# Four of the eight transfers of the first w_in piece issued from ScalarE's queue instead of SyncE's

## The chip, the core and the metric

The kernel runs on one NeuronCore of a Trainium2 chip. The metric is the device time of one execution in microseconds (us), the median of several runs. The core has five engines with an instruction stream each: TensorE (PE; its weight loads are shown as PEld), VectorE (DVE), ScalarE (ACT), GpSimd (POOL) and SyncE (SP). In this kernel transfers from and to memory are issued from SP's stream and, for a few, from ACT's.

## The reference

A gated linear recurrence over 4 batches of 8 heads, 768 steps, 48 features, and a feed-forward block on its output (3072 tokens of 384 features, 2048 hidden).

```python
state = np.zeros((B, H, D, D), dtype=np.float32)
for t in range(S):
    state = alpha[:, :, t, :, None] * state + np.einsum('bhd,bhe->bhde', k[:, :, t], v[:, :, t])
    y[:, :, t] = np.einsum('bhd,bhde->bhe', q[:, :, t], state)
...
x = np.ascontiguousarray(y.transpose(0, 2, 1, 3)).reshape(B * S, H * D)
h = x @ w_in
g = h - np.tanh(h)
return (g @ w_out).astype(np.float32)
```

The weights w_in and w_out come as 64-bit floating point numbers; all else is 32-bit.

## The kernel before, in words

The tokens are worked in 12 units of 256 (`TU`), three to a batch. Each unit has two parts. The recurrence (`gla`) turns alpha, k and q so that features lie on partitions, scans alpha from both ends on DVE (`scan_U` L711, `scan_W` L730), scales k by U and q by W (`times` L679), and then for each chunk of 128 tokens forms scores on PE (`scores`), masks them on DVE (`masked`), multiplies by v (`products`) and updates the state. The feed-forward part (`moe`) runs 8 steps per unit: `first` (six matmuls with w_in, L1081, out tile h), four operations on ACT and DVE that form g, and `second` (matmuls with w_out, L1126 for units 0 and 1, L1147 with fewer products from unit 2 on). Unit 0's and 1's steps are numbered 0 to 15 here in the order in which they run.

The weights arrive in 16 pieces during unit 0 and 1's work. A piece of w_in is eight transfers (six of 48 partitions, two of 16), one of w_out is one; `load_weight` (L39 to L44) issues them, all on SP. A piece holds raw 64-bit numbers; `round_weight` makes 32-bit ones of them with two operations on ACT (L86, L87) and two on DVE (L89, L90), here called the conversion of the piece. It writes the tile `w_in[:, :, 2*s*128 : 2*(s+1)*128]`, that is a stretch in each of three rows j, which interleave with those of other pieces.

At the very start the eight loads of unit 0's alpha, k, q and v are issued in halves, one half each from SP and ACT (L595, L584). Then SP goes on with the first piece of w_in (L43), unit 1's alpha (L600), the second piece, and so on. The program gives eight semaphores to these transfers in turn, so that each transfer waits until the one that had its semaphore before has landed. ACT's stream holds, after its four loads, a table load and a small wake-up operation (L478), then the copy of alpha's first half out of PSUM into tile aT (`place`, L670); DVE copies the second half into the same tile, alternate columns of it.

The order of all this is not written by hand. Every piece of work is a task with an engine, an estimated time, a rank and the tasks that it needs. `Planner.order` simulates the engines with these estimates, eight times with changed priorities, keeps the best plan and emits the tasks in the order of their planned starts; each engine runs its own in that order. `plan.begin` (L1211) says at what time each engine is free for planned work. Where the plan leaves PE idle ahead of the first products (task "y 0.0"), `spin` (L1209) fills in matmuls of the identity with itself, one for each 0.24 us of planned idle time.

The task `fetch` (L566) of a piece carries the time that its issues are thought to take on SP: 5.7 for the first two pieces, 4.3 for later ones of w_in, 2.0 for w_out.

Of the kernel before, what the change touches and what calls it, by code (L numbers as in the profile page):

```python
# [35 lines left out]
R_MAX = 2.0 ** 60  # L36


def load_weight(nc, pool, rows, **kw):  # L39

    raw = pool.tile([P, WN], I64 if rows[0][2].dtype != FP32 else FP32, name="raw", **kw)
    for at, js, src in rows:
        nc.sync.dma_start(out=raw[at].rearrange("p (j n) -> p j n", n=src.shape[-1])[:, js], in_=src)  # L43
    return raw  # L44


def weight_parts(w_in, w_out, pad_rows, what, s, by_tile=True):

    if what == "out":
        return [(slice(0, P), slice(0, 2), w_out.rearrange("(j p) n -> p j n", p=P)[:, 2 * s:2 * s + 2, :])]  # L50
    parts = []
    for i in range(len(pad_rows[0])):
        at, f0 = pad_rows[0][i]
        step = pad_rows[1][i][1] - f0
        src = w_in[f0:f0 + len(pad_rows) * step].rearrange("(j p) n -> p j n", p=step)
        src = src[0:at.stop - at.start, :, 2 * s * P:2 * (s + 1) * P]

        few = at.stop - at.start < 32 or not by_tile
        parts += [(0, at, slice(0, len(pad_rows)), src)] if few else [(j - 9, at, slice(j, j + 1), src[:, j:j + 1]) for j in range(len(pad_rows))]
    return [x[1:] for x in sorted(parts, key=lambda x: (x[0], x[1].start))]  # L60
# [73 lines left out]
def general(tc, q, k, v, alpha, moe_w_in, moe_w_out, out, w_in, w_out, ident, pad_rows):  # L134
# [10 lines left out]
    with ExitStack() as ctx:  # L145
        with tc.tile_pool(name="g_raw", bufs=1) as raw_pool:
            for s in range(FT // 2):
                for what, dst in (("in", w_in[:, :, 2 * s * P:2 * (s + 1) * P]), ("out", w_out[:, 2 * s:2 * s + 2, :])):
                    raw = load_weight(nc, raw_pool, weight_parts(moe_w_in, moe_w_out, pad_rows, what, s))
                    round_any_weight(nc, raw_pool, raw, dst)  # L150
# [171 lines left out]
class Planner:  # L322
# [13 lines left out]
    def add(self, name, engine, us, rank, after, do, lat=0.3):  # L336
        kind = name.rsplit(" ", 1)[0]
        self.tasks.append((name, engine, us, rank, [a for a in after if a], do, lat, self.last.get(kind)))
        self.last[kind] = name
# [85 lines left out]
def fast(tc, q, k, v, alpha, moe_w_in, moe_w_out, out, w_in, w_out, ident, ok, pad_rows):  # L425
    nc = tc.nc
# [12 lines left out]
    V, A, T, GP = nc.vector, nc.scalar, nc.tensor, nc.gpsimd  # L439
# [3 lines left out]
    with ExitStack() as ctx:  # L443
# [7 lines left out]
        raw_pool = incoming.enter_context(tc.tile_pool(name="incoming", bufs=2))  # L451
# [83 lines left out]
        plan = Planner()  # L535
        add = plan.add
# [11 lines left out]
        pieces = sorted(((what, s) for s in range(FS) for what in RANK), key=lambda x: (RANK[x[0]] + 2 * x[1], x))  # L548
        raw_of = {}

        def fetch(what, s):
            raw_of[what, s] = load_weight(nc, raw_pool, weight_parts(moe_w_in, moe_w_out, pad_rows, what, s), bufs=4)

        def convert(what, s):
            it = []

            def begin():
                dst = w_in[:, :, 2 * s * P:2 * (s + 1) * P] if what == "in" else w_out[:, 2 * s:2 * s + 2, :]
                it.append(round_weight(nc, raw_pool, raw_of.pop((what, s)), dst))
                next(it[0])  # L560
            return begin, lambda: next(it[0], None)

        for n, (what, s) in enumerate(pieces):
            rank = RANK[what] + 2 * s
            held = pieces[n - 4] if n >= 4 else None
            add(f"fetch {what}{s}", "SP", 5.7 if n < 2 else 4.3 if what == "in" else 2.0, rank - 30, [held and f"read {held[0]}{held[1]}"],  # L566
                lambda what=what, s=s: fetch(what, s), lat=2.5)
            a, b = convert(what, s)
            older = pieces[n - 2] if n >= 2 else None
            add(f"read {what}{s}", "ACT", 1.9, rank, [f"fetch {what}{s}", older and f"{older[0]}{older[1]}"], a)  # L570
            add(f"{what}{s}", "DVE", 1.6, rank, [f"read {what}{s}"], b)
# [480 lines left out]
        def reload(n):  # L1052
            looked[n] = load_weight(nc, combo_pool[0], weight_parts(moe_w_in, moe_w_out, pad_rows, *pieces[n], by_tile=False))
# [4 lines left out]
        for n in range(len(pieces)):  # L1058
            rank = 2 * FS * 3 + 8 * n
# [148 lines left out]
                spun.append(ps_o.tile([P, P], FP32, name="spin", tag="o2"))  # L1208
            T.matmul(spun[0], lhsT=ident, rhs=ident, start=True, stop=True)  # L1209
        plan.filler = "PE", "y 0.0", 0.24, spin  # L1210
        plan.begin.update(SP=0.8, PE=1.5, ACT=3.0, DVE=4.8)  # L1211

        for u in range(NU):
            gla(u, rank_gla(u))
# [44 lines left out]
def kernel(  # L1259
# [28 lines left out]
    w_out = consts.tile([P, FT, d_model], FP32, name="w_out")  # L1288
    ok = consts.tile([1, 1], I32, name="ok")
    fine = fast(tc, q, k, v, alpha, moe_w_in, moe_w_out, out, w_in, w_out, ident, ok, pad_rows)  # L1290
    with tc.If(fine < 1):
        general(tc, q, k, v, alpha, moe_w_in, moe_w_out, out, w_in, w_out, ident, pad_rows)
# [30 lines left out]
```

## Time and profile before

| what | us |
|---|---|
| median of 3 runs (lowest, highest) | 578.11 (577.57, 578.14) |
| the profiled execution's own time | 578.14 |
| its span in the profile | 576.4 |
| PE busy, share of the span | 568.0, 99% |
| DVE busy | 451.0, 78% |
| ACT busy | 322.8, 56% |
| first matmul of `first` (L1081) starts at | 31.23 |
| fillers (L1209) before that, matmuls | 46 |

In the profile a 32-bit matmul shows as two records, so that 18 fillers are "x36". Times in its rows are us from the start of the span. A row of the timeline gives the start, the length, the engine, the line, the operation with its tiles and shapes, how many are merged, and in brackets how long the engine sat idle before and what ended that. "SPq" and "ACTq" are issues of transfers from the streams of SP and ACT.

### The profile page before, as it was taken

To read this page: it belongs to the slowest core of one execution; us is meant where nothing else is said; L and a number is where in the kernel's file an instruction comes from. 1 tells how busy PE (TensorE), PEld (TensorE's weight loads), DVE (VectorE), ACT (ScalarE), POOL (GpSimd) and SP (SyncE) were. 2 spreads that over 40 slices of the span, in tenths; PEclk is the share of its full clock that TensorE was granted. 3 is DMA by queue.
4 is the path that set the end of the run, shared out by engine and by line. 5 is a ranking of instruction groups with operands and counts; after the bars stand their busy time and mean duration, and the time that the engine had idled before them with its cause. 6 is when DMAs were issued, how large, how long until landed. Compare 5 with 4: busy or idle time off the path is not lost.

```text
span 576.4 us, 13857 instructions
## 1 busy us (share of the span) xinstructions
PE 568.0 (99%) x5637; PEld 503.6 (87%) x5637; DVE 451.0 (78%) x886; ACT 322.8 (56%) x559; POOL 4.8 (1%) x22
## 2 busy tenths in 40 slices
PE   8999999999999999999999999999999999999995
PEld 8887777778989999998999999899998999899995
DVE  5989879999999995896895896896797645554643
ACT  2589985737768686577485365264443433333531
POOL 3000000000000000000000000000000000000000
PEclk9999999999999999999999999999999999999998
DMA  8888791235673762562630320310200000000001
GB/s 185 199 232 237 244 177 56 84 74 128 121 159 114 141 142 85 118 156 77 183 113 2 85 61 2 74 51 23 56 8 1 30 8 2 28 8 1 27 2 34
DMA packets 60713, 50.84 MB, mean 88 GB/s; under 512 B 35776, under 2 KB 50400, under 8 KB 60640
## 3 DMA queue, kind: packets, MB, share of 16 engines
q1 hardware_dynamic: 57728, 48.88, 34.3%
q10 hardware_dynamic: 2912, 0.98, 0.8%
q8 instruction: 46, 0.75, 0.6%
q14 instruction: 27, 0.22, 0.1%
HBM read 44.04 MB, written 4.72 MB: 85 GB/s over the span
## 4 chain that ended last, share of the span: by engine, by line
PE 96%; DMA 1%; DVE 1%; ACT 1%; issue 0%; SPq 0%; POOL 0%; DVEq 0%; POOLq 0%
PE h L1081 42%; PE o L1147 32%; PE o L1126 7%; PE sc L806 2%; PE spin L1209 2%; PE sc L879 2%; PE sc L889 2%; PE sc L812 2%; PE sc L992 1%; DMA raw<-in_moe_w_in_dram 1%; PE turned L663 1%; PE scores L796 0%; PE sc L663 0%; PE y L854 0%; PE y L861 0%
## 5 line engine op out<-in xcount | busy, mean ns | idle before, releaser
L1081 PE MATMUL h<-xT,w_in 128*128 128x256 f32 x1152 | 265.1, 381 | 0.2 <-DVE w_in L90 0.2
L1081 PEld LDWEIGHTS h<-xT,w_in 128*128 128x128 f32 x1152 | 216.0, 190 | 27.1 <-DVE w_in L90 0.3
L1090 ACT ACTIVATE u<-h 128x512 f32<-128x512 f32 x96 | 56.9, 593 | 181.5 <-PE h L1081 181.0
L1098 DVE TENSOR_TENSOR w<-h,u 128x512 f32<-128x512 f32 x96 | 65.9, 687 | 79.0 <-ACT u L1090 78.7
L1147 PE MATMUL o<-b,e 128*128 128x192 f32 x480 | 90.9, 327 | 0.0
L1147 PE MATMUL o<-w_out,e 128*128 128x192 f32 x320 | 81.5, 337 | 0.0
L1147 PEld LDWEIGHTS o<-b,e 128*128 128x128 f32 x480 | 80.2, 191 | 0.0
L1102 DVE SCALAR_TENSOR_TENSOR g<-z,w 128x512 f32<-128x512 f32 x96 | 65.6, 684 | 4.4 <-PE o L1126 1.3
L1147 PE MATMUL o<-b,g 128*128 128x192 f32 x320 | 65.1, 327 | 0.0
L1094 ACT ACTIVATE z<-u 128x512 f32<-128x512 f32 x96 | 60.4, 629 | 2.6
L1147 PEld LDWEIGHTS o<-w_out,e 128*128 128x128 f32 x320 | 55.8, 190 | 4.3
L1147 PEld LDWEIGHTS o<-b,g 128*128 128x128 f32 x320 | 54.2, 191 | 0.0
L1108 ACT ACTIVATE big<-u 128x1024 f32<-128x1024 f32 x48 | 50.4, 1049 | 0.0
L1126 PE MATMUL o<-w_out,g 128*128 128x384 f32 x128 | 44.0, 488 | 0.0
L1126 PEld LDWEIGHTS o<-w_out,g 128*128 128x128 f32 x128 | 24.1, 190 | 13.7
L1114 DVE TENSOR_TENSOR e<-g 128x256 f32<-128x256 f32 x80 | 33.6, 420 | 1.8
L1115 DVE TENSOR_TENSOR e<-g 128x256 f32<-128x256 f32 x80 | 33.4, 417 | 0.0
L639 DVE STREAM_TRANSPOSE aT<-ar 128x256 f32<-128x256 f32 x44 | 28.4, 645 | 2.8 <-ACT ar L633 1.7
L730 DVE TENSOR_TENSOR_SCAN W<-aT,before 128x1032 f32<-128x1032 f32 (+1 forms) x13 | 27.7, 2133 | 0.0
L711 DVE TENSOR_TENSOR_SCAN U<-aT,after 128x1032 f32<-128x1032 f32 (+1 forms) x13 | 27.6, 2132 | 0.1
L1116 DVE TENSOR_TENSOR e<-g 128x128 f32<-128x128 f32 x80 | 22.8, 285 | 0.0
L639 DVE STREAM_TRANSPOSE qT<-qr 128x256 f32<-128x256 f32 x40 | 20.5, 634 | 0.0
(138 smaller groups left out, 566.2 us busy)
## 6 DMA issues: line engine op xcount, KB each, us to landing
raw<-in_moe_w_out_dram SPq DMA_DIRECT2D x16, 768.0 KB, 5.0
raw<-in_moe_w_in_dram SPq DMA_DIRECT2D x80, 96.0 KB, 4.1
raw<-in_moe_w_in_dram SPq DMA_DIRECT2D x16, 288.0 KB, 4.8
vt<-in_v_dram SPq DMA_DIRECT2D x23, 192.0 KB, 4.3
ar<-in_alpha_dram SPq DMA_DIRECT2D x44, 96.0 KB, 3.1
kr<-in_k_dram SPq DMA_DIRECT2D x40, 96.0 KB, 2.2
qr<-in_q_dram SPq DMA_DIRECT2D x40, 96.0 KB, 2.3
out_dram<-cross SPq DMA_DIRECT2D x19, 96.0 KB, 1.7
```

Source lines behind the costliest of these rows:

```text
L639: V.transpose(to, raws[what][:, g, :, 0:32])
L730: V.tensor_tensor_scan(out=m["W"][:, ns].rearrange("p n t -> p (n t)"), data0=aT[:, a:z], data1=before[:, a:z], initial=0.0, op0=ALU.mult, ...
L1081: T.matmul(h[:, a, :], lhsT=w_in[:, j, f * P:(f + 1) * P], rhs=xT[u][:, j, :], start=(j == 0), stop=(j == KT - 1))
L1090: A.activation(m["u", s], m["h", s], AF.Square, scale=W_SCALE ** -1.5)
L1094: A.activation(m["z", s], m["u", s], AF.Square, bias=QB, scale=QA * W_SCALE)
L1098: V.tensor_mul(m["w", s], m["h", s], m["u", s])
L1102: V.scalar_tensor_tensor(out=g.rearrange("p a c t -> p (a c t)"), in0=m["z", s], scalar=QK, in1=m["w", s], op0=ALU.add, op1=ALU.mult)
L1108: A.activation(big, m["us", s // 2].rearrange("p s t -> p (s t)"), AF.Relu, bias=-U_FAST, scale=W_SCALE, accum_out=over[:, n:n + 1])
L1114: V.tensor_add(e[:, 0:2, :], g[:, 0], g[:, 1])
L1115: V.tensor_sub(e[:, 2:4, :], g[:, :, 1, :], g[:, :, 0, :])
L1126: T.matmul(m["o"][c], lhsT=g[:, a, c, :], rhs=w_out[:, f, :], start=(f == 0), stop=(f == FT - 1))
L1147: T.matmul(o[n][:, i], lhsT=g_, rhs=w_, start=(s_ == 0 and (n, i) in ((0, 0), (1, 0), (2, 1), (3, 0))), stop=(s_ == FS - 1), skip_group_ch ...
```

## The change

`load_weight` can take a list of queues and issues its transfers from them in turn. The first piece (the earliest in the plan, w_in's first) gets ACT and SP, so that each issues four of its eight transfers. All other pieces stay on SP. The planner is told 3.0 us of SP for the first piece in place of 5.7, 5.0 for the second in place of 5.7, and that ACT is free from 5.4 us on in place of 3.0. As the planner works with these numbers, the order of tasks on all engines changes in the early part.

```diff
-def load_weight(nc, pool, rows, **kw):
+def load_weight(nc, pool, rows, queues=None, **kw):
...
-    for at, js, src in rows:
-        nc.sync.dma_start(out=raw[at].rearrange("p (j n) -> p j n", n=src.shape[-1])[:, js], in_=src)
+    for n, (at, js, src) in enumerate(rows):
+        (queues[n % len(queues)] if queues else nc.sync).dma_start(out=raw[at].rearrange("p (j n) -> p j n", n=src.shape[-1])[:, js], in_=src)
...
-            raw_of[what, s] = load_weight(nc, raw_pool, weight_parts(moe_w_in, moe_w_out, pad_rows, what, s), bufs=4)
+            raw_of[what, s] = load_weight(nc, raw_pool, weight_parts(moe_w_in, moe_w_out, pad_rows, what, s),
+                                          queues=[A, nc.sync] if (what, s) == pieces[0] else None, bufs=4)
...
-            add(f"fetch {what}{s}", "SP", 5.7 if n < 2 else 4.3 if what == "in" else 2.0, rank - 30, [held and f"read {held[0]}{held[1]}"],
+            add(f"fetch {what}{s}", "SP", 3.0 if n == 0 else 5.0 if n == 1 else 4.3 if what == "in" else 2.0, rank - 30, [held and f"read {held[0]}{held[1]}"],
...
-        plan.begin.update(SP=0.8, PE=1.5, ACT=3.0, DVE=4.8)
+        plan.begin.update(SP=0.8, PE=1.5, ACT=5.4, DVE=4.8)
```

Line numbers after L552 are higher by one in the changed kernel.

In the built programs the early orders differ as follows.

| engine | before | after |
|---|---|---|
| ACT | wake-up, copy of alpha, v's gap copy, size of U, k's turned copy, w_in conversion 0, ... | wake-up, four issues of the first piece, copy of alpha, v's gap copy, size of U, w_in conversion 0, k's turned copy, ... |
| SP, after the eight loads | piece 0 (8 issues), unit 1's alpha (4), piece 1 (8), unit 1's k and q (4), piece 2 (8) | piece 0 (4), piece 1 (8), unit 1's alpha (4), piece 2 (8), unit 1's k and q (4), piece 3 (8) |
| DVE, after the work on U, W, k and q | w_in conversion, masks of chunks 0 and 1, unit 1's turning of alpha, its U, w_in conversion | masks of chunks 0 and 1, w_in conversion, unit 1's turning of alpha, w_in conversion, its U, w_in conversion |
| PE, fillers in each stretch | 18, 6, 6, 6, 2, 8 | 18, 6, 11 |

From step 11 on PE's order is the same in both.

## The prediction

> **What bounds the kernel now.** First the page's busy times and chain of waits, then the time by stages: after the start TensorE (PE) is never idle, so a change can only act through what PE waits for early on, the fillers it runs there (spin, L1209), and the cost of changing between shapes of matmul.
>
> ```profile
> PE 568.0 (99%) x5637; PEld 503.6 (87%) x5637; DVE 451.0 (78%) x886; ACT 322.8 (56%) x559; POOL 4.8 (1%) x22
> ...
> 12.00:31.20 19.20, 19.10 (x268) 17.14 (x262) 18.08 (x39) 11.83 (x22) 0.00 (x0) 1.00 0.81 196
> 31.20:50.00 18.80, 18.59 (x260) 14.74 (x262) 15.68 (x24) 16.39 (x27) 0.00 (x0) 1.00 0.82 230
> ...
> 100.00:560.00 460.00, 460.00 (x4613) 415.00 (x4612) 362.79 (x720) 248.21 (x443) 0.00 (x0) 1.00 0.28 68
> ```
>
> The columns are PE, PEld, DVE, ACT, POOL busy, clock, DMA. From 12 to 31.2 us VectorE (DVE) is 94% busy too: that stage hangs on DVE's chain, and PE's fullness there is partly filler. So I read DVE, ScalarE (ACT) and the SP queue in order of time.
>
> ```profile
> 2.48 0.53 ACTq L584 DMA_DIRECT2D vt<-in_v_dram  x1
> 3.04 1.28 ACT L478 ACT_TABLE_LOAD   x1 [3.04 <-issue]
> 4.82 0.20 ACT L478 ACTIVATE wake<-wake 128x1 f32<-128x1 f32 x1 [0.50 <-DVE wake L477]
> 8.73 0.65 ACT L670 COPY aT<-turned 128x512 f32<-128x512 f32 x1 [3.71 <-PE turned L663]
> ...
> 9.62 0.69 DVE L670 COPY aT<-turned 128x512 f32<-128x512 f32 x1 [4.85 <-PE turned L663]
> 10.41 2.36 DVE L711 TENSOR_TENSOR_SCAN U<-aT,after 128x516 f32<-128x516 f32 x2
> ...
> 4.59 6.68 SPq L43 DMA_DIRECT2D raw<-in_moe_w_in_dram  x8
> 10.48 0.80 SPq L43 DMA_DIRECT2D raw<-in_moe_w_in_dram  x2
> SPq L43 <- DMA vt<-in_v_dram: 2.0, 1, 2.0
> SPq L43 <- DMA rough<-in_alpha_dram: 1.7, 1, 1.7
> SPq L43 <- DMA rough<-in_q_dram: 0.8, 1, 0.8
> SPq L43 <- DMA rough<-in_k_dram: 0.6, 1, 0.6
> ```
>
> Two things to see. ACT issues DMAs in its own order: its table load waits until the fourth issue is over (2.48 + 0.53). And SP's eight issues of the first w_in piece need 6.68 us because each reuses the semaphore of one of the eight first loads and waits for that load to land; the seventh waits 2.0 us, until v's second half lands at 10.46.
>
> **The change, part by part.** *Four of the eight transfers go to ACT.* In the built program they stand behind the wake-up (done 5.02) and ahead of ACT's copy of alpha (L670). Their waits are for ACT's halves of k, q and v, then for SP's half of v; SP's four wait for alpha, alpha, k and q. So ACT's third issue cannot start before 10.48, the row in which SP waited for that landing, and its fourth follows: two issues, 0.80 by SP's row (1.1 by ACT's own issues of 0.53). ACT's copy starts at 11.3 (11.6) in place of 8.73. Behind it on ACT stand only the v gap copy and the size of U, which has slack; but DVE's copy of alpha's other half writes alternate columns of the same tile and waits for ACT's. It now starts at 11.3 + 0.65 = 12.0, not 9.62, and U at 12.0 + 0.79 = 12.8, not 10.41: **2.4 us late**.
>
> *The first piece comes no earlier:* its last transfers are still issued after 10.48. It landed in time before (ACT read it at 15.38 behind a DVE-bound operation); that gain is 0. SP gets to the second piece at about 10.3 instead of 13.88 and to unit 1's alpha, k, q some 3 us later (alpha's issues 11.32 before, about 15 now; k's 17.69, about 21). Landing 3.6 to 6.1 us after issue, as q's did, q is there by 28 to 29.8 and PE wants it at 28.5 to 30.3; a delay there lies under the wait of PE below, so 0 (up to 0.5 if that wait were not there).
>
> The Trainium skill, "DMA: Bandwidth & Descriptors", section "Issuing engines are not separate DMA queues", says that a second issuing engine saves only the sequencer's issuing time. Here that would be four issues of 0.38 us, 1.5 us of SP, and SP's other 3.6 us were waits that the rule gives no relief from; it speaks against this change, as the rows do.
>
> *The planner's costs (3.0, 5.0, ACT from 5.4) change the order.* They cost nothing themselves. From step 11 of the MLP on (the first matmul of it at 91.17 before) PE's order is the same as before, so I sum up to there.
>
> DVE's order, with start-to-start times from rows of before: U at 12.8; up to the end of the 17 operations on U, W, k and q 7.76 (10.41 to 18.17) gives 20.56; state 0.30; four masks 2.42 (19.74 to 20.93, 21.25 to 22.48) and 0.3 for the second scores; the first w_in conversion, now behind the masks, 1.57 (18.17 to 19.74); state 0.27; four transposes and a memset 2.65; second conversion 1.55; unit 1's U 2.22; third conversion 0.67 + 0.97. Sum **33.5**.
>
> PE meets that. The second matmul of step 0 (j = 1) waits in the built program for the last w_in conversion written before it, since the pieces interleave over j: the second one before, the third now. PE gets to step 0 at about 31.3, much as before (31.23): it has waited 1.9 us for k (14.25 to 16.15), and has 17 fillers where there were 28 after 12.9 (11 x 0.22 = 2.5 us), 8 more turns of q (0.9), and fewer changes to and from the filler (0.2 each, the 0.64 for two spins at 19.42 shows one). So at the second matmul it waits about 1.8 and starts at 33.55 in place of 31.55: **+2.0**.
>
> ```profile
> 31.23 5.45 PE L1081 MATMUL h<-xT,w_in 128*128 128x256 f32 x24
> 36.60 1.09 PE L663 MATMUL sc<-ident,rough 128*64 128x128 f32 x16
> 42.61 2.86 PE L1081 MATMUL h<-xT,w_in 128*128 128x256 f32 x12 [0.21 <-DVE w_in L90]
> ```
>
> From there to step 11: the turn of q that went ahead is gone from 36.60, **-1.3** (1.03, and 0.30 for getting into it: 2.89 in place of 2.59 for the step before). Two blocks of narrow matmuls now follow each other, which saves changes of shape: 0.2 to 0.4 each (2.79 against 2.59 for a step that precedes one), **-0.6** in all. The 0.21 at 42.61 goes, **-0.2**. And step 3's second matmul waits anew: DVE goes on from 33.5 with 0.97 (ends, k), W 2.21, k, q, cube, q 2.4, a w_out conversion 1.5, shrunk 0.6, and a w_in conversion that must wait for step 2 on PE (42 + 0.9), then seven operations of 2.84 in all and the next conversion 1.64: 47.3. PE is there at 33.55 + 2.2 + 2.6 + 0.8 + 2.8 + 1.1 + 2.6 = 45.6, plus 0.4: **+1.3**.
>
> Sum: 2.0 - 1.3 - 0.6 - 0.2 + 1.3 = **+1.2, of which I take 1.1**, since the same addition along before's order comes out 0.1 to 0.3 late at its first h. The profiled execution took 578.14 (span 576.4 and 1.7 around it), the median is 578.11: 579.2.
>
> **A cost the trace doesn't show: the clock after a wait.** PE has no wait over 0.4 us between its start and its end, so none shows what waits of 1.9, 1.8 and 1.3 us do. The nearest rows are the tail, where PE's last matmul ended at 569.84, and the start.
>
> ```profile
> 570.00:572.00 2.00, 0.00 (x0) 0.00 (x0) 0.56 (x1) 0.00 (x0) 0.00 (x0) 0.97 0.60 188
> 572.00:576.40 4.40, 0.00 (x0) 0.00 (x0) 0.00 (x0) 0.00 (x0) 0.00 (x0) 0.50 0.06 19
> 1.57 3.78 PE L1209 MATMUL spin<-ident 128*128 128x128 f32 x16 [1.57 <-POOL ident masks.py:199]
> 5.43 2.17 PE L1209 MATMUL spin<-ident 128*128 128x128 f32 x18
> ```
>
> The clock 0.97 over 2 us and then 0.50 means that it fell at 571.9, 2.1 us after PE stopped. At the start 16 records took 3.78 us and 18 then 2.17: half speed for some 3.7 us. So one drop costs from 0 to 1.85 us, on the path in either place. I take 0 (our waits are shorter than 2.1) and keep 1.85 for the range.
>
> The same skill, "TensorE: Matmul & The Clock Gate", section "What's actually happening", has the clock halved after an idle window of about 3.4 us that runs freely. By it our waits are too short and the sum is unchanged; the tail's 2.1 us says that less can be enough.
>
> **Rivals.**
> *ACT is not held* (chance 0.15): v lands earlier, or ACT's issues do not block its copy. Against it: 10.48 and 3.04 in the rows above. Then U starts at 10.5, the third conversion ends at 31.2, PE's second matmul of step 0 starts about as before or 0.2 sooner, and the rest of the sum (-0.8) stands: 577.2 (576.7 to 577.7). This is the side on which it is not slower; it decides if ACT's copy starts before 9.5.
> *The clock falls in one of the long waits* (0.23): 579.2 + 1.85 = 581.0; two falls 582.9. It decides if a wait reaches some 2 us, and the first is 1.9. For it: the tail. Against it: PE is busy again within the same few us.
> *The conversions do not hold PE* (0.07): if the waits of steps 0 and 3 were gone, PE would start step 0 at 31.3 and the sum is 0.1 - 1.3 - 0.6 - 0.2: 576.1. Against it: the 0.21 wait on w_in at 42.61 is of this very kind.
> The forecast (0.55) by itself: 578.4 to 580.2, from its three waits at 0.3 each and ACT's issues at 0.80 or 1.1.
>
> **How the numbers follow.** 0.2% (1.16 us) is about what a measurement of this kernel can tell from no change, so the bounds are 576.95 and 579.27. The forecast lies just inside: half of its 0.55 is slower, half within. The clock rival is slower; of the unheld ACT two thirds are within and a third faster; the last rival is faster. Slower 0.27 + 0.23 = 0.50; within 0.28 + 0.10 = 0.38; faster 0.05 + 0.07 = 0.12. The range leaves out the last rival, the lower part of the first and the double clock fall: 577.2 to 581.2.
>
> **What would show it.** Right: ACT's four issues end near 11.3, its copy of alpha starts there, U at 12.8; PE waits about 1.9 us ahead of the first turning back of k near 16, and at steps 0 and 3 on w_in's conversion; 17 fillers after 12.9. Wrong: U at or before 10.6; step 0's matmuls in one piece at 31; a granted clock under 1 between 14 and 40; or a wait in steps after 11, where I have none.

## The result, and the profile after

The changed kernel took 580.28 us in the median of 4 runs (579.97 to 580.83), the kernel before 577.84 beside it (4 runs): ratio 1.0044, 95% interval 1.0026 to 1.0061, so it is slower by some 2.4 us. The profiled executions are 580.15 (span 578.4) and 578.14 (span 576.4), 2.0 apart.

First the rows of the windows view of the changed kernel that answer to those of the prediction (PE, PEld, DVE, ACT, POOL busy, granted clock, share of the DMA engines, GB/s):

```profile
12.00:31.20 19.20, 17.02 (x256) 15.09 (x254) 17.97 (x35) 12.29 (x22) 0.00 (x0) 1.00 0.79 193
31.20:50.00 18.80, 15.88 (x136) 12.24 (x132) 17.91 (x30) 16.57 (x24) 0.00 (x0) 1.00 0.95 255
```

PE lost 2.1 us of busy time in the first stage (19.10 before) and 2.7 in the second (18.59 before). Part of what went is work (11 fillers fewer, a turn of q gone ahead), the rest is waiting. DVE is as full as it was, or fuller. The clock stays at 1.00. Which waits they are, the timelines of ACT, DVE and PE of the changed kernel tell:

```profile
6.16 5.60 ACTq L43 DMA_DIRECT2D raw<-in_moe_w_in_dram  x4
11.87 0.64 ACT L671 COPY aT<-turned 128x512 f32<-128x512 f32 x1 [6.84 <-DMA raw<-in_moe_w_in_dram]
12.54 0.69 DVE L671 COPY aT<-turned 128x512 f32<-128x512 f32 x1 [7.77 <-ACT aT L671]
13.33 2.36 DVE L712 TENSOR_TENSOR_SCAN U<-aT,after 128x516 f32<-128x516 f32 x2
...
16.65 0.60 PE L927 MATMUL y<-ident,kT 112*128 112x112 f32 x4 [2.19 <-DVE kT L680]
...
31.56 0.70 PE L1082 MATMUL h<-xT,w_in 128*128 128x256 f32 x2
33.98 5.02 PE L1082 MATMUL h<-xT,w_in 128*128 128x256 f32 x22 [1.71 <-DVE w_in L90]
...
46.05 0.59 PE L1082 MATMUL h<-xT,w_in 128*128 128x256 f32 x2
47.85 2.43 PE L1082 MATMUL h<-xT,w_in 128*128 128x256 f32 x10 [1.21 <-DVE w_in L90]
```

The brackets read upwards: step 0 and step 3 wait for DVE's conversions, the first kT for DVE, DVE's copy for ACT's copy, and that for ACT's own issues, which last from 6.16 to 11.76 (its bracket counts them as idle time and names the transfers that they start). U starts at 13.33 in place of 10.41. The chain of waits says the same. Its first long pieces (start, length, what) were, before,

```profile
1.57 6.03 PE spin L1209 x36
7.60 2.77 PE turned L663 x48
```

and in the changed kernel

```profile
1.34 4.81 DMA rough<-in_k_dram
6.16 5.71 DMA raw<-in_moe_w_in_dram
11.87 0.64 ACT aT L671
12.54 0.70 DVE aT L671
13.33 1.29 DVE U L712 x2
```

The beginning of the kernel no longer hangs on PE's first turns but on ACT's four issues (the 5.71 of raw), the third of which starts at 10.97, when v's half has landed. Along PE's order, by the starts of the weight loads, the second matmul of step 0 is 2.43 later than before, step 11 is 1.67 later at its first matmul and 1.89 at its second, and at the last step (559.60 against 557.71) the distance is 1.89 again.

### The profile page after: what moved, and what is told of

Its sections match the earlier page's. It is cut to its first block, busy times and chain, and to the rows that moved or that the text cites. A ratio compares the mean times of both kernels' runs of the same rounds, so it can differ in the third digit from the quotient of the medians.

```text
span 578.4 us, 13800 instructions
## 1 busy us (share of the span) xinstructions
PE 565.1 (98%) x5615; PEld 500.1 (86%) x5615; DVE 450.8 (78%) x886; ACT 322.7 (56%) x559; POOL 4.8 (1%) x22
## 3 DMA queue, kind: packets, MB, share of 16 engines
q10 hardware_dynamic: 3168, 1.38, 1.1%
HBM read 44.04 MB, written 4.72 MB: 84 GB/s over the span
## 4 chain that ended last, share of the span: by engine, by line
PE 92%; DMA 4%; DVE 2%; ACT 1%; issue 1%; SPq 0%; ACTq 0%; DVEq 0%
PE h L1082 42%; PE o L1148 32%; PE o L1127 7%; PE sc L807 2%; PE sc L880 2%; DMA raw<-in_moe_w_in_dram 2%; DMA rough<-in_k_dram 2%; PE sc L890 2%; PE sc L813 2%; PE sc L993 1%; DVE U L712 1%; PE spin L1210 0%; SPq L43 0%; DVE w_in L90 0%; PE y L880 0%
```

## The experiments

The theory: four issues stand ahead of ACT's copy of alpha, the last two of them wait for v, U is late by that, and DVE's late conversions then hold PE. Its rivals: the new order costs, or moving the first piece over two queues does, wherever its issues stand. Each run was timed beside the kernel before on the same chip. The table has, of each profiled execution, the start of PE's first turn of alpha (L663/L664), the start of U, PE's wait ahead of the first turning back of k, the second matmuls of steps 0 and 3, the first of step 11 (all three by the start of the weight load, up to 0.3 ahead of the matmul), and its time; the ratio with its interval is that of all runs.

| kernel | first turn | U | wait | step 0 | step 3 | step 11 | us | ratio to before |
|---|---|---|---|---|---|---|---|---|
| before | 7.53 | 10.41 | 0 | 31.55 | 42.93 | 91.17 | 578.14 | 1 |
| changed | 7.47 | 13.33 | 2.19 | 33.98 | 47.85 | 92.84 | 580.15 | 1.0044 (1.0026, 1.0061) |
| e1 order alone | 7.82 | 10.71 | 0 | 31.89 | 45.76 | 91.36 | 579.49 | 1.0003 (0.9994, 1.0011) |
| e2 split alone | 8.57 | 13.27 | 1.03 | 33.83 | 45.21 | 93.45 | 580.19 | 1.0042 (1.0029, 1.0054) |
| e3 issues behind | 8.28 | 11.17 | 0 | 38.73 | 52.59 | 97.59 | 584.90 | 1.0122 (1.0108, 1.0137) |
| e4 pieces apart | 8.45 | 13.31 | 1.19 | 32.14 | 45.66 | 90.77 | 578.33 | 1.0034 (1.0021, 1.0046) |
| e5 two on ACT | 8.48 | 11.36 | 0 | 32.59 | 46.47 | 91.46 | 578.48 | 1.0011 (1.0000, 1.0021) |
| e6 DVE copies | 8.66 | 11.47 | 0 | 33.27 | 47.14 | 92.34 | 579.82 | 1.0031 (1.0016, 1.0046) |
| e7 changed, again | 7.44 | 13.40 | 2.29 | 34.05 | 47.92 | 92.91 | 580.04 | 1.0038 (1.0023, 1.0052) |
| e8 pieces, again | 7.27 | 14.80 | 3.86 | 34.99 | 48.78 | 94.19 | 581.75 | 1.0023 (1.0006, 1.0039) |
| e9 last two | 8.70 | 13.05 | 0.67 | 33.70 | 47.58 | 92.57 | 579.90 | 1.0024 (1.0013, 1.0036) |
| e10 order + pieces | 8.36 | 11.25 | 0 | 30.42 | 44.15 | 91.00 | 578.60 | 0.9980 (0.9971, 0.9990) |
| e11 before + pieces | 7.35 | 10.24 | 0 | 31.37 | 42.36 | 90.60 | 577.35 | 0.9992 (0.9983, 1.0001) |
| e12 order + pieces, again | 8.32 | 11.21 | 0 | 31.15 | 44.11 | 91.85 | 579.51 | 0.9995 (0.9985, 1.0005) |

**The two halves of the change (e1, e2).** e1 keeps the planner's numbers and takes the split away, e2 keeps the split and takes the numbers away.

```diff
 e1:
-                                          queues=[A, nc.sync] if (what, s) == pieces[0] else None, bufs=4)
+                                          queues=None, bufs=4)
 e2:
-3.0 if n == 0 else 5.0 if n == 1 else 4.3 if what == "in" else 2.0
+5.7 if n < 2 else 4.3 if what == "in" else 2.0
...
-        plan.begin.update(SP=0.8, PE=1.5, ACT=5.4, DVE=4.8)
+        plan.begin.update(SP=0.8, PE=1.5, ACT=3.0, DVE=4.8)
```

> The new order without the split: all eight transfers of the first piece stay on SP, the planner keeps the changed numbers, so PE, DVE and the rest of ACT run in the changed kernel's order. Theory (the four issues ahead of ACT's copy of alpha are the loss): ACT copies alpha near 8.7, U starts near 10.4, the wait for kT ahead of the first turning back of k is gone, the third w_in conversion ends 2.9 us earlier than in the changed kernel (33.92 - 2.92 = 31.0), step 0's second matmul starts near 31.1 and step 3's near 45.0; profiled time 580.15 - 2.9 = 577.2, that is 0.9 below the kernel before. Rival order (the new order itself is slow): 579.9 to 580.5, as the changed kernel. Rival transfers (two queues moving the first piece are slow, not the hold on ACT): also near 577.2, so this run separates the order from the split only.

> The split without the new numbers: ACT issues four of the eight transfers, the planner's costs are those of before, so the order is that of before, fillers 28 after 12.9 included. Theory: U at 13.3 as in the changed kernel, a wait of about 2.2 us on kT near 16.6, and with all 28 fillers still in the stream step 0 starts at 31.23 + 2.2 = 33.4 or a little later; profiled time 578.14 + 2.2 to 2.9 = 580.3 to 581.0. Rival order: as the kernel before, 577.8 to 578.5. Rival transfers: 579.5 or more, without saying where.

The split alone costs what the whole change costs (1.0042 against 1.0044), with U at 13.27 and fillers as before; its wait for kT is 1.03, not the expected 2.2, since PE's own first turn came 1.04 later than in the kernel before. The order alone is level with the kernel before (1.0003), so the rival that blames the order falls. But it gained nothing, where 0.9 was expected; three lines of PE's timeline of e1 show where that went:

```profile
31.89 5.02 PE L1082 MATMUL h<-xT,w_in 128*128 128x256 f32 x22 [0.79 <-DVE w_in L90]
...
88.27 0.98 PE L993 MATMUL sc<-ident,kT 112*128 112x112 f32 x8 [0.39 <-DVE kT L736]
...
142.83 2.86 PE L1082 MATMUL h<-xT,w_in 128*128 128x256 f32 x12 [0.24 <-DVE w L1099]
```

Step 0's wait is still there, shorter, and two waits on DVE that neither parent has stand farther down; the last (0.24, and a restart) takes PE from 0.4 behind the kernel before to 0.9 behind.

**The issues behind the copy (e3).** ACT's four issues were emitted after its copy of alpha.

```diff
+        if queues is not None and n % 2 == 0:
+            queues.append(issue)
...
+                if u == 0 and n == 0:
+                    for issue in held_back:
+                        issue(A)
```

> The changed kernel with ACT's four issues moved behind its copy of alpha; everything else, the order on PE and DVE too, is the changed kernel's. Theory: ACT's copy at 8.7, U at 10.4, ACT's issues end near 11 to 12 as before and nothing waits for what stands behind them (the gap copy of v is wanted by PE at 23.6); from there as in the order alone: profiled time 577.2 (576.7 to 577.8). Rival transfers: the first piece still comes over two queues, so 579.5 to 580.5. Rival order: 579.9 to 580.5.

U came with the first turn again (11.17), but the time rose by 1.2%, which no theory had. ACT's and PE's timelines of e3, then its windows:

```profile
11.96 2.54 ACTq L43 DMA_DIRECT2D raw<-in_moe_w_in_dram  x4
...
18.98 1.06 ACT L90 ACTIVATE more<-raw 128x768 int16<-128x768 uint32 x1 [3.10 <-DMA ar<-in_alpha_dram]
19.91 1.03 ACT L91 ACTIVATE more<-raw 128x768 f16<-128x768 f32 x1
20.81 0.51 ACT L940 COPY kn<-y 128x448 f32<-128x448 f32 x1
...
21.37 1.09 PE L948 MATMUL y<-vt,kn 128*64 128x48 f32 x16 [3.24 <-ACT kn L940]
22.39 2.08 PE L805 MATMUL scores<-qT,kT 48*128 48x128 f32 x16
```

```profile
17.07:20.48 3.41, 1.06 (x10) 0.87 (x8) 1.93 (x5) 1.50 (x2) 0.00 (x0) 1.00 0.60 153
20.48:30.72 10.24, 9.35 (x90) 7.93 (x92) 4.88 (x10) 6.16 (x12) 0.00 (x0) 0.50 0.86 214
30.72:34.00 3.28, 3.28 (x58) 2.53 (x56) 3.14 (x7) 2.48 (x3) 0.00 (x0) 1.00 0.90 255
```

Emitted later, the issues got other semaphores of the eight: each now waited for a transfer that SP had issued in the meantime, the last for one that landed at 14.15, and landed itself at 18.88. ACT read the piece at 18.98 (the bracket names a transfer of ar; the read needs the piece), and kn is behind that read on ACT. PE waited 3.24 us, and the clock (the column ahead of the DMA share) was at half from 20.48 to 30.72. The scores (x16) took 2.08 where they took 1.16 before. So e3 says nothing about the split; it moved the wait to the piece itself, and showed what a long wait of PE costs.

**Which issues hold ACT (e5, e9).** Both put two of the eight transfers on ACT: e5 the two that reuse semaphores of k and q, e9 two of which the second reuses that of v's half.

```diff
 e5:
+queues=[A, nc.sync, A, nc.sync] + [nc.sync] * 4 if (what, s) == pieces[0] else None
 e9:
+queues=[nc.sync, nc.sync, nc.sync, nc.sync, nc.sync, nc.sync, A, A] if (what, s) == pieces[0] else None
```

> The changed kernel with only two of the eight transfers on ACT, the two that reuse the semaphores of ACT's halves of k and q; the two that waited for v go back to SP. Order as in the changed kernel. Theory (it is the wait for v ahead of the copy that costs): ACT's second issue follows the landing of q's half (7.80 in the changed kernel's trace) and ends by 8.5, ACT copies alpha at 8.7 to 9.0, U at 10.4 to 10.7, no wait for the first kT; the time as with the order alone, ratio to the kernel before 0.999 to 1.001. Rival transfers (a first piece moved from two queues is what costs): half of the loss or more stays, 1.002 to 1.004.

> Two of the eight transfers on ACT as in the run with two, but the last two: ACT's second issue now reuses the semaphore of v's half in place of q's. Number of issues on ACT, number of queues and the planner's numbers are those of the run with two. Theory (the wait for v ahead of the copy): ACT's second issue starts after v's half lands (10.9 to 11.5) and ends 0.3 to 0.45 later, ACT's copy near 11.3 to 12, U at 12.7 to 13.4, a wait for the first kT of 1.5 to 2.3; ratio to the kernel before 1.0025 to 1.004. Rival transfers (issues or queues as such): as the run with two, 1.000 to 1.002, U at 10.4 to 11.4.

ACT's timeline of e5, then that of e9:

```profile
6.25 1.90 ACTq L43 DMA_DIRECT2D raw<-in_moe_w_in_dram  x2
9.68 0.64 ACT L671 COPY aT<-turned 128x512 f32<-128x512 f32 x1 [4.65 <-PE turned L664]
```

```profile
6.27 5.21 ACTq L43 DMA_DIRECT2D raw<-in_moe_w_in_dram  x2
11.58 0.64 ACT L671 COPY aT<-turned 128x512 f32<-128x512 f32 x1 [6.55 <-PE turned L664]
```

As many issues from as many queues, with the same numbers for the planner: e5's are over at 8.15 and its copy waits for PE's turn, e9's last until 11.48, when v is there, and the copy starts 1.90 later. The bracket of e9 names PE, though the turns that the copy needs were over by then (in e5 the copy follows the first turn by 1.20, which would be 9.90 here): it is a row in which the last releaser is to be looked for in the line above. e5 is at 1.0011, e9 at 1.0024, each 0.0001 outside the range of its theory on the side of the other; the intervals overlap, so it is the rows that tell the two apart (U at 11.36 and 13.05, step 11 at 91.46 and 92.57). e9's wait for kT was 0.67, not 1.5 to 2.3, since PE's first turn came at 8.70. What holds ACT's copy is the wait for v, not the number of queues.

**The copy taken from ACT (e6).** All four issues stay on ACT; DVE copies both halves of alpha.

```diff
-                (V.tensor_copy if n else A.copy)(gc(tail[:, :, 0:P])
+                V.tensor_copy(gc(tail[:, :, 0:P])
```

> The changed kernel, all four issues on ACT where they are, but alpha's first half is copied by DVE too (one row of 0.69 more on DVE, one of 0.64 less on ACT). Theory: nobody on the chain waits for ACT any more; DVE copies the first half near 8.8, the second near 9.6, U at 10.4 to 10.8, ACT's issues still end near 11.8; ratio to the kernel before 0.999 to 1.0015. Rival transfers: 1.003 to 1.005, since the transfers are those of the changed kernel.

U is free (11.47, 2.81 after the first turn), and yet the ratio was 1.0031, where the theory had at most 1.0015 and the rival 1.003 to 1.005. ACT's timeline of e6:

```profile
6.26 6.94 ACTq L43 DMA_DIRECT2D raw<-in_moe_w_in_dram  x4
...
16.53 1.09 ACT L86 ACTIVATE more<-raw 128x768 int16<-128x768 uint32 x1 [1.51 <-DMA raw<-in_moe_w_in_dram]
17.47 1.05 ACT L87 ACTIVATE more<-raw 128x768 f16<-128x768 f32 x1
18.39 0.50 ACT L932 COPY kn<-y 128x448 f32<-128x448 f32 x1
```

ACT's fourth issue itself took 1.58 here (0.44 in the changed kernel's profile). The piece landed at 16.4, ACT's read of it waited 1.51, and kn behind the read came at 18.39, against 16.68 in e5. PE waited 0.43 for kn and DVE 0.79 for ACT's state; step 11 stands 0.88 behind that of e5, with a first turn 0.18 later. So the split has a second cost, a late first piece, that is hidden as long as U is late too; its last transfer stands behind the wait for v as well (ACT's third issue started at 11.26). How much of e6's 1.0031 it makes in the other executions isn't shown. With all four issues on ACT the rival "transfers" is thus not excluded by e6; against it speaks that e5, where two of the eight also come from ACT, has lost most of the loss (1.0011), and e9, with as many from ACT and the wait for v, has more of it (1.0024).

**The false wait on the conversions (e4, e8; e10, e11, e12).** w_in is laid out by pieces, so that no conversion of a later piece overlaps what a step reads; e4 and e8 are the changed kernel with it, e11 the kernel before, e10 and e12 the order alone.

```diff
-    w_in = consts.tile([P, KT, d_ff], FP32, name="w_in")
+    w_in = consts.tile([P, d_ff // (2 * P), KT, 2 * P], FP32, name="w_in")
...
-                dst = w_in[:, :, 2 * s * P:2 * (s + 1) * P] if what == "in" else w_out[:, 2 * s:2 * s + 2, :]
+                dst = w_in[:, s] if what == "in" else w_out[:, 2 * s:2 * s + 2, :]
...
-lhsT=w_in[:, j, f * P:(f + 1) * P]
+lhsT=w_in[:, f // 2, j, f % 2 * P:(f % 2 + 1) * P]
```

> The changed kernel with w_in laid out so that each piece is one contiguous stretch (step, row j, column) and conversions of later pieces no longer overlap what an earlier step reads. Issues, order and U (13.3) stay. Theory: step 0's and step 3's second matmuls no longer wait for a w_in conversion, step 0 runs in one piece from 31.56, saving 2.1; DVE is as late as before, so some of it comes back as a wait for kT or cube near 37 to 39 (the second kT product of unit 1 ends at 37.67, PE would be there at 37.0: 0.7). Step 3's wait of 1.2 goes too. Profiled time 580.15 - 1.0 to 2.6 = 577.5 to 579.1. Rival (the conversions do not hold PE, something else does): unchanged at 580.1, the same starts of step 0's second matmul.

> The changed kernel with w_in's pieces laid out apart, a second time, because its profiled execution (578.33) lay 2.2 below the median of its runs. If the waits at steps 0 and 3 are worth what the trace showed (step 11 at 90.77 in place of 92.84, end 1.6 earlier), ratio to the kernel before 1.000 to 1.002 and some 1.5 us below the changed kernel beside it. If the profiled execution was an exception: 1.003 to 1.005, level with the changed kernel, and the trace should show a longer wait for kT or a lower clock.

> The order alone (all transfers on SP) with w_in's pieces laid out apart. The order alone waited 0.79 at step 0, 1.20 at step 3 and 0.39 at 88.3 for unit 2's kT. Theory: the first two waits go and PE reaches 88 up to 2.0 earlier, but kT there comes from DVE, which does not, so the third wait grows by what the first two give; step 11 at 90.5 to 91.4, ratio to the kernel before 0.998 to 1.000. Rival (nothing later holds PE): step 11 at 89.4, ratio 0.9965 to 0.9975.

> The kernel before with w_in's pieces laid out apart and nothing else. Theory: its order has only one wait on a w_in conversion (0.21 at step 3), so at most 0.2 is gained: ratio to the kernel before 0.9992 to 1.0003, and the gain of the run with order and pieces together needs both. Rival (the layout by itself is faster, in DVE's writes or PE's reads): ratio near 0.998.

> Order and pieces together a second time, beside the pieces alone. Theory: ratio to the kernel before 0.9970 to 0.9990 again. Rival (the first measurement was luck of early landings): 0.9992 or more.

In e4 steps 0 and 3 run in one piece:

```profile
31.82 5.45 PE L1082 MATMUL h<-xT,w_in 128*128 128x256 f32 x24
...
45.44 2.75 PE L1082 MATMUL h<-xT,w_in 128*128 128x256 f32 x12
```

With U as late as in the changed kernel, step 11 comes at 90.77 in place of 92.84 and the last step at 558.03 in place of 559.60. The two waits were real, and in this execution they were worth 2.07 at step 11 and 1.57 at the end. But over all runs e4 and e8 are at 1.0034 and 1.0023 and spread from 577.82 to 582.33, and e8's profile shows why the same kernel can take 3.4 us more. ACT's and PE's timelines of e8:

```profile
6.51 6.73 ACTq L43 DMA_DIRECT2D raw<-in_moe_w_in_dram  x4
13.35 0.63 ACT L671 COPY aT<-turned 128x512 f32<-128x512 f32 x1 [8.32 <-DMA raw<-in_moe_w_in_dram]
...
18.12 0.82 PE L927 MATMUL y<-ident,kT 112*128 112x112 f32 x4 [3.86 <-DVE kT L680]
18.73 4.09 PE L1210 MATMUL spin<-ident 128*128 128x128 f32 x22
```

ACT's fourth issue took 1.32, U started at 14.80, PE waited 3.86, and the clock fell: 11 fillers took 4.09 in place of 2.63.

The mean granted clock on record for each execution tells how often that happened. It is 0.996 or more in all 87 executions of the kernel before beside e1 to e12, and in all 58 of e1, e5, e10, e11 and e12. The profiles of e3 and e8, in which the clock fell on the way, have 0.989 and 0.995. A value of 0.995 or less, read as such a fall, stands beside 5 of 12 executions of e8 (580.64 to 582.33), all 4 of e3, 3 of 11 of e9, 2 of 6 of e6, and one each of e2, e4 and e7. The other seven of e8 have a median of 578.71, the other five of e7, the changed kernel beside it, 580.04. So where the clock holds, the layout gives the changed kernel some 1.3 us, near the 1.5 that e8's theory had; it doesn't keep the clock from falling.

The order with pieces apart was at 0.9980 in e10, below the kernel before, but at 0.9995 in e12, where the rival (luck) was put; with the pieces alone e11 is at 0.9992, its interval reaching 1.0001. So a gain over the kernel before isn't established for any of them, while e10 to e12 all lie below the changed kernel. What the pieces free in e10 meets the next wait:

```profile
36.20 0.99 PE L993 MATMUL y<-ident,kT 112*128 112x112 f32 x8 [0.66 <-DVE kT L680]
...
87.91 0.98 PE L993 MATMUL sc<-ident,kT 112*128 112x112 f32 x8 [0.90 <-DVE kT L736]
```

**The changed kernel once more (e7).**

> The changed kernel itself on the chip of the runs beside it. Theory: ratio to the kernel before 1.003 to 1.005, U near 13.3, a wait of 2.0 to 2.4 us for kT, 1.7 at step 0 and 1.2 at step 3, granted clock 1.00 throughout. Rival clock: if the wait for kT comes out over 2.4 us, the clock falls after it as it did in the run with the issues behind the copy (3.24 us of wait, 0.50 until about 30), and the time is some 4 us higher.

1.0038, U at 13.40, a wait of 2.29 for kT and no fall of the clock in the profiled execution: as in the first measurement. One of its six executions (581.97, mean clock 0.995 where the others have 0.997) is the clock rival's case.

**What the table shows at a glance.** Wherever ACT isn't held and copies its half itself (before, e1, e3, e5, e10, e11, e12), U starts 2.88 or 2.89 after PE's first turn. Wherever it is held (changed, e2, e4, e7, e8, e9), U starts 1.56 or 1.57 after the end of ACT's issues (11.76, 11.71, 11.74, 11.83, 13.24, 11.48), whatever PE does, though the first turn moved from 7.27 to 8.70. That is the theory in two constants. The loss in a single execution is the difference of the two, and changes with both.

## Why the prediction was right, and where it was off

- *ACT held by its issues, U late: right, and mis-sized by 0.5.* The copy was put at 11.3 (11.6), U at 12.8; they came at 11.87 and 13.33. The step reckoned v's landing at 10.48, from the row of before; in the changed kernel's trace v's half landed at 10.95, and the issues were over at 11.76, not at 11.3. In the 14 profiles that landing lies between 10.46 and 11.54, and the one used was the earliest of all. This is the term that failed in size.
- *The first piece lands no earlier: right.* Its last transfer landed at 15.6 in place of 14.44, and ACT read it at 16.79 in place of 15.38. That it could come late enough to hold kn (e6) was not among the terms.
- *The waits: right in place.* kT 1.9 predicted, 2.19 measured; at step 0 1.8 and 1.71, at step 3 1.3 and 1.21. As DVE is late, they end 0.43 and 0.55 later than predicted: step 0's second matmul 33.55 and 33.98, step 3's 47.3 and 47.85. The fillers were the 17 named.
- *The sum.* +1.2 (1.1 taken) was worked out to step 11; +1.89 came. Of the 0.7 too little, 0.43 stands at step 0's second matmul: U was 0.53 later than predicted, and the way from U to there 20.65 in place of the predicted 20.75. In the changed kernel, e7 and e9 it is 20.65 each time, so a later U is passed on whole. The rest, some 0.26 between there and step 11, is not taken apart. The medians are 2.44 apart, more than twice the 1.1 of the sum: 580.28 lies just above the forecast's own 578.4 to 580.2 and within the stated range only because that was widened for a fall of the clock, which the four executions measured here do not show. So the mechanism was right, and that the number stayed in the range was in part luck.
- *The rival "ACT is not held": its condition was refuted by the changed kernel, its price by e1.* e1 is that case, with U at 10.71, and measured 1.0003, not the 577.2 of the sum. The third conversion was put at 31.2 and ended at 31.84: the first turn was 0.3 later, and DVE, now ahead, waited 0.83 in all for scores and state from PE and ACT ahead of its masks. The waits at 88.27 and 142.83 took more. So the gains listed for the order (-1.3, -0.6, -0.2) came to nothing in the whole: each wait of the three lines of e1 ends on DVE, which has no room to follow.
- *The rival "the clock falls": absent in both profiles of the changed kernel* (1.00 in each window, with waits of 2.19 and 2.29), *but the mechanism is real and close by.* By the mean clock one of the changed kernel's ten executions (581.97) has it. That the others have not isn't because the waits are under 2.1, as the prediction took it, for they are over; it hung on where they fell (see the last section). It fell in e3 and e8. Its price was bounded by 1.85; e8 paid 1.7 (1.46 on the fillers, 0.22 on the L927 group before them), e3 4.2 (its seven slow groups from L948 at 21.37 to L870 at 29.79, 10.15 in all, against 5.97 for the same groups in the changed kernel). The upper bound was wrong, since it took the length of the start's slow stretch (3.7) for the length of any; e3's lasted 10.24.
- *The rival "the conversions do not hold PE": refuted by e4*, where the waits at steps 0 and 3 are gone.

## What to carry to other kernels

An issue that must wait for its semaphore holds everything behind it on its engine: before moving transfers to a compute engine's stream, look for whose landing each of them waits and what that engine computes next. Where a wait is removed, ask first what the engine that ended it does next; here the order alone gained nothing, since DVE had no room. And a tile whose pieces interleave makes a reader wait for a writer of another piece, so pieces that are written at different times should lie apart; here that was worth some 1.3 us where an order had such waits, and is not shown to pay where it had not (e11).

## What the runs showed of the hardware

- *When the clock falls.* In the clock records of the 14 traces every finished stretch at one granted clock lasts a whole multiple of 3.413 us (3.41 in e8, 10.24 in e3, 13.65 in both, 549.55 to 570.03 for the long ones). So the clock changes on a grid of such windows, whose place differs from execution to execution. From full speed it fell at the end of every window in which PE was busy for 1.38 us or less (40%), and after none in which it was busy for 1.49 or more (44%). The rows of such windows, one of e8, one of the tail of before, and two of the tail of e2, where the second is the one that ends in a fall:

```profile
14.96:18.37 3.41, 0.24 (x2) 0.25 (x3) 3.38 (x7) 1.18 (x3) 0.00 (x0) 1.00 0.80 189
568.46:571.87 3.41, 1.38 (x9) 1.08 (x7) 2.03 (x4) 0.00 (x0) 0.00 (x0) 1.00 0.33 101
570.64:574.05 3.41, 1.49 (x10) 1.19 (x8) 2.04 (x4) 0.06 (x1) 0.00 (x0) 1.00 0.31 98
574.05:577.46 3.41, 0.00 (x0) 0.00 (x0) 0.00 (x0) 0.00 (x0) 0.00 (x0) 1.00 0.15 44
```

So the fall came 2.1 us after PE stopped in the tail of before, 2.4 in e3, and 4.1 in e8, when PE was already at work again. The waits of 2.19 and 2.29 in the changed kernel and e7 were split between two windows, in each of which PE was busy for 59% or more. A window at half clock costs half its length if PE is busy throughout, 1.7 us, which is what e8 paid. The Trainium skill, "TensorE: Matmul & The Clock Gate", section "What's actually happening", has a window of about 3.4 us that runs freely, and the clock halved after an idle one. The grid agrees with the first; on the second the runs decide, since windows in which PE was busy for up to 40% were enough.
- *The start scatters.* The last 27 records of the leading fillers began at 3.65 in every profile and took from 3.69 (e8) to 5.12 (e9), so PE's first turn moved by 1.4 us and, where nothing else holds it, U with it. The spacing of these records halves, from 0.21 to 0.11, where the trace's clock record begins, at 4.72 in e8 and 7.72 in e9: it is the grid again.
- *One issue near 12 us is held.* In most profiles an issue between 3 and 11 us takes 0.31 to 0.47; in each of the 14 one that starts between 11.36 and 12.47 takes 1.0 to 1.6 and ends between 12.6 and 13.9. Why is not shown. Before, it was SP's second of unit 1's alpha (1.11). When it is ACT's fourth (1.58 in e6, 1.32 in e8), ACT pays.
